# The mask product in four 32-column pieces, and the unread products at routing's end in 64-row halves

## The chip, the cores and the metric

The kernel runs on one core of a Trainium2 chip. A core has a matrix engine (TensorE, PE in the profile, with its weight loads as PEld), VectorE (DVE), ScalarE (ACT), GpSimd (POOL) and SyncE (SP), which issues most of the DMA transfers. The metric is the device time of one execution in microseconds (us); lower is better. Three runs of the kernel before took 480.1, 476.44 and 481.21 us, a median of 480.1.

## What is computed

An attention over 8 batches of 8 heads, 576 positions and 64 channels is the sum of two softmax attentions. One works on queries, keys and values averaged over groups of four positions, and its result is repeated four times. The other is local: a position sees only positions less than four away. The result, 4608 rows of 512, goes through a layer of experts. A row whose skip score is positive goes to the expert of its largest logit and adds that expert's two-layer output, weighed by the softmax of its logits; the other rows stay as they are.

```python
mask = np.abs(pos[:, None] - pos[None, :]) < factor          # factor = 4
scores = scale * np.matmul(q, k.transpose(0, 1, 3, 2))
scores = np.where(mask, scores, -1000000000.0)
...
out[do_compute] = xc + y      # y = gate * relu(xc @ w1[e]) @ w2[e]
```

## The kernel before

**Attention.** The 4608 rows are cut into 36 tiles of 128, each made of four groups of 32 positions. A group sees a window of 38 keys, so a tile's local scores are 128 x 304 (8 heads of 38) in one bank of PSUM, a tile S of which there are two. `scores` (line 409) makes them: first one product of the bf16 identity `idb` with the mask `mk`, 128 x 128 weights and 304 moving columns, which writes zeros and large negative numbers into the whole bank; then 16 products in fp32, for four pairs of heads and four groups, each with 32 columns of weights, that add queries times keys into their 32 partitions. A product in fp32 shows in the trace as two passes, so the 16 stand there as x32. `s_max` and `s_sub` on VectorE read the bank. The averaged attention (names ending in d: KD, qd, Ed, PTd), the values (`O<-VB,PT`, `O<-vd,PTd`, products of 32 columns) and the repeated result (`O<-U,rep`, full products) are mixed between.

**Order.** All steps up to the experts are entries of a list (`node`), and the table `ORDER` says in which order they are written. PE, ACT and DVE, and likewise POOL and SP, carry them out in that order, each engine in its own queue. Loads of the next batch are tied to the product that was written last ahead of them (`paced`), so that the queue of SP waits for PE.

**Routing.** After every 16 tiles, and once more after the last four, `route` turns the logits into lists of rows for each expert. On VectorE the last call finds each row's expert (oh), counts (on PE, `Sd<-oh,tri` and `Sd<-oh,ones`), makes the slot of each row (sl, s_all, blk, smod, ok), the number of rows of each expert (cnt), and two factors of a list product, Am and Bm. PE multiplies them (`Sd<-Bm,Am`), VectorE adds the result to ids and writes gix, the row numbers by expert. With gix POOL fetches the rows of the first expert (`xr<-out,gix`, three fetches of 128 rows), PE transposes them, ACT and DVE split them in two, and the experts' products begin. Gate weights follow the same way in a second list product with 72 columns.

**Unread products.** Among these last steps stand four entries `warm_s` (line 911), which multiply a tile of ones by itself into a bank S whose content nobody reads, 2, 2, 4 and 4 times with 512 columns (`WARM`). Behind the table's part 14 more of the kind stand between the first transposes (`WARMX`, into `py`).

**Steps that the table does not place.** Behind the experts the kernel has a branch for experts with more than 384 rows. Its condition is worked out by five VectorE steps, nf and nb (lines 1088 to 1092), from cnt. They are written after the hand-set order ends, and the planner of the language puts them where its own reckoning of time suggests; in the kernel before they stand among the steps that make gix.

Of the kernel before, what the change touches and what calls it, by code (L numbers as in the profile page):

```python
# [12 lines left out]
F32 = mybir.dt.float32  # L13
# [9 lines left out]
H, SEQ, HD = 8, 576, 64  # L23
E, D, F = 8, 512, 1024
QG, KW = 32, 38
# [7 lines left out]
WV = KS * KR  # L33
CAP = 384
NBK = CAP // 128
WARM = (2, 2, 4, 4)
WARMX = (5, 4, 3, 2)
SR = 8192
C_RANK, C_COL, C_BASE, C_SP8, C_SP4, C_SP2 = 0, 8, 32, 48, 56, 60
# [83 lines left out]
def tile_attention_moe(ctx, tc, qT, kT, vW, v4, mask, cst, ups, cid, w9, w1, w2, out):  # L123
    nc = tc.nc
# [3 lines left out]
    def pool(stack, name, bufs, **kw):  # L128
        return stack.enter_context(tc.tile_pool(name=name, bufs=bufs, **kw))
# [5 lines left out]
    ident = cp.tile([128, 128], F32, name="ident")  # L135
# [17 lines left out]
    psS = pool(att, "psS", 2, space=PSUM)  # L153
# [6 lines left out]
    mk = kvp.tile([128, 4, KW], BF16, name="mk")  # L160
    idb = kvp.tile([128, 128], BF16, name="idb")
# [15 lines left out]
    quad = [slice(32 * j, 32 * j + 32) for j in range(4)]  # L177
# [16 lines left out]
    def mm(*args, **kw):  # L194
        last[:] = [nc.tensor.matmul(*args, **kw)]  # L195
# [213 lines left out]
    def scores(i):  # L409
        S = psS.tile([128, 512], F32, name="S")  # L410
        Sv = TT[i]["S"] = S[:, :H * KW].rearrange("p (h k) -> p h k", h=H)
        v = MASKS.get(i % 9, 0)
        mm(Sv, lhsT=idb, rhs=mk[:, v:v + 1, :].to_broadcast([128, H, KW]), start=True, stop=False)
        for p in range(4):
            for j, b, g in groups(i):
                o, k = SEQ * p + QG * g, KO + SEQ * p + QG * g - 3
                mm(Sv[quad[j], 2 * p:2 * p + 2], lhsT=B[b]["Q"][:, o:o + QG],
                                 rhs=KBs[b % 2][:, :, k:k + KW], start=False, stop=p == 3)
# [338 lines left out]
    def node(fn, *args):  # L757
        nodes.append((fn, args))
# [55 lines left out]
    for b in range(NB):  # L814
# [39 lines left out]
        for i in range(NTILE):  # L854
            if (4 * i + 3) // NG != b:
                continue
            if i % 2 == 0 and i > 0:
                for r in range(2):
                    node(load_v, i // 2, r)
            node(scores, i)  # L860
            node(s_max, i)
            node(s_sub, i)
# [19 lines left out]
            if i % RG == RG - 1 or i == NTILE - 1:  # L882
                n = i % RG + 1
# [23 lines left out]
    def warm(t, n):  # L907
        for _ in range(n):
            nc.tensor.matmul(t, lhsT=ones, rhs=ones[:, None, :].to_broadcast([128, 4, 128]), start=True, stop=True)

    def warm_s(n):
        warm(psS.tile([128, 512], F32, name="S"), n)

    for e in range(2):
        node(load_n, e)
    for n in WARM:
        node(warm_s, n)
# [176 lines left out]
    with tc.If(some > 0):  # L1094
# [11 lines left out]
        for e in range(E):  # L1106
            n_blk = nc.values_load(nb[0:1, e:e + 1], engines=engines, min_val=0, max_val=(NTOK - CAP + 127) // 128)
            with tc.If(n_blk > 0):
# [7 lines left out]
                with tc.For_i(0, n_blk, 1) as it:  # L1116
# [14 lines left out]
                    for f in range(8):  # L1131
                        ph = psV.tile([128, 512], F32, name="pho")
                        for c in range(4):
                            nc.tensor.matmul(ph[:, :128], lhsT=w1t[:, f // 2, c, 128 * (f % 2):128 * (f % 2) + 128],
                                             rhs=xt[:, c, :], start=c == 0, stop=c == 3)
# [78 lines left out]
```

## Time and profile before

| | |
|---|---|
| three timed runs | 480.1, 476.44, 481.21 us |
| the profiled execution | 477.29 us |
| its span, from first to last instruction | 475.5 us |
| granted TensorE clock, mean over the span | 0.983 of full |
| PE busy | 437.1 us (92%) |
| DVE busy | 314.8 us (66%) |
| ACT busy | 252.9 us (53%) |
| POOL busy | 169.8 us (36%) |

Busy shares are means over stages: attention lasts until about 197 us, routing's end until about 226 us, the experts until the end. A product's time in the trace runs from its first column to the end of its result, and the next product starts well before that, so that what a product costs PE is read from start to start.

### The profile page before, as it was taken

The page shows a single profiled execution, that of the slowest core. Times are in us where ns is not written, and L with a number is a line of the kernel's source. Part 1 is how long each engine was busy: PE and PEld are TensorE (multiplying, and loading weights), DVE is VectorE, ACT ScalarE, POOL GpSimd, SP SyncE. Part 2 cuts the span into 40 slices and gives each one's busy share as a digit, 9 for nine tenths or more (in the row PEclk, how much of TensorE's full clock was granted, in tenths as well). Part 3 has the DMA queues.
Part 4 walks back from the last instruction along what each step waited for, and adds up shares of the span by engine and source line. Part 5 has one row for each costly group of instructions (what it writes and reads, how often), then busy time and mean ns, then how long its engine had stood idle before and what let it go on. Part 6 is the DMA issues. An engine that isn't in the chain of part 4 may idle for free. (4 is left out here: it accounts for less than half of the span.)

```text
span 475.5 us, 13311 instructions
## 1 busy us (share of the span) xinstructions
PE 437.1 (92%) x5461; PEld 366.6 (77%) x5461; DVE 314.8 (66%) x573; ACT 252.9 (53%) x585; POOL 169.8 (36%) x191
## 2 busy tenths in 40 slices
PE   0879989899999999997999999999999999999990
PEld 0557767678787777783898989989989899899880
DVE  4899987668779879575546555546686644776330
ACT  7547777587767678643443443344646334363210
POOL 8575967346567346005200502304131220202001
PEclk9989999999999999997999999999999999999997
DMA  7888879788898786653835544645776664555101
GB/s 259 275 257 272 278 230 287 217 253 299 253 287 282 222 252 221 176 180 107 274 132 179 206 142 152 197 161 163 244 225 241 204 214 130 181 180 193 47 4 60
DMA packets 27116, 96.71 MB, mean 203 GB/s; under 512 B 4245, under 2 KB 4629, under 8 KB 24618
## 3 DMA queue, kind: packets, MB, share of 16 engines
q1 hardware_dynamic: 23186, 84.36, 56.3%
q0 software_dynamic: 3840, 11.09, 6.4%
q8 instruction: 64, 1.05, 0.9%
q14 instruction: 26, 0.21, 0.1%
HBM read 81.20 MB, written 15.73 MB: 204 GB/s over the span
## 5 line engine op out<-in xcount | busy, mean ns | idle before, releaser
L958 POOL DMA_INDIRECT out<-Y,six x24 | 24.2, 1010 | 189.9 <-DVE Y L1018 188.1
L991 PE MATMUL ph<-xth,w1h 128*128 128x384 f32 (+2 forms) x256 | 80.6, 315 | 0.3 <-ACT xth L982 0.3
L991 PE MATMUL ph<-xtl,w1h 128*128 128x384 f32 (+2 forms) x256 | 78.9, 308 | 0.3 <-DVE xtl L983 0.3
L991 PE MATMUL ph<-xth,w1l 128*128 128x384 f32 (+2 forms) x256 | 78.8, 308 | 0.0
L1011 PE MATMUL py<-w2h,hh 128*128 128x512 f32 x168 | 66.1, 394 | 0.4
L1011 PE MATMUL py<-w2h,hl 128*128 128x512 f32 x168 | 65.7, 391 | 0.0
L1011 PE MATMUL py<-w2l,hh 128*128 128x512 f32 x168 | 65.5, 390 | 0.0
L1000 ACT ACTIVATE hh<-ph 128x384 fp32r<-128x384 f32 x64 | 30.7, 490 | 55.4 <-PE py L1011 27.8
L1001 DVE SCALAR_TENSOR_TENSOR hl<-ph,hh 128x384 fp32r<-128x384 f32 x64 | 34.7, 554 | 35.3 <-ACT hh L1000 35.3
L991 PEld LDWEIGHTS ph<-xth,w1h 128*128 128x128 f32 x256 | 48.1, 188 | 1.2 <-ACT xth L982 0.8
L991 PEld LDWEIGHTS ph<-xtl,w1h 128*128 128x128 f32 x256 | 48.3, 188 | 0.9 <-DVE xtl L983 0.5
L991 PEld LDWEIGHTS ph<-xth,w1l 128*128 128x128 f32 x256 | 48.1, 188 | 0.0
L288 DVE TENSOR_REDUCE KD<-KB 128x288 f32<-128x1152 f32 (+1 forms) x36 | 42.7, 1209 | 7.1 <-DMA KB<-kT 7.0
L709 DVE TENSOR_TENSOR w2l<-raw,w2h 128x1024 fp32r<-128x1024 f32 x32 | 39.1, 1221 | 10.4 <-ACT w2h L708 10.4
L982 ACT CAST xth<-Tx 128x512 fp32r<-128x512 f32 x22 | 13.0, 590 | 59.9 <-PE Tx L977 59.9
L747 DVE TENSOR_TENSOR w1l<-raw,w1h 128x1024 fp32r<-128x1024 f32 x30 | 36.7, 1225 | 7.8 <-ACT w1h L742 7.8
L445 POOL TENSOR_TENSOR Nt<-Et,r 128x304 f32<-128x304 f32 x36 | 25.9, 724 | 43.4 <-DVE r L442 12.6
L708 ACT CAST w2h<-raw 128x1024 fp32r<-128x1024 f32 x32 | 33.6, 1050 | 14.3 <-PE py L1011 14.3
L195 PE MATMUL O<-VB,PT 126*32 126x128 f32 x1152 | 38.6, 275 | 1.5 <-DMA VB<-vW 1.0
L195 PE MATMUL Sd<-KD,qd 128*128 128x288 f32 (+1 forms) x128 | 27.3, 422 | 13.1 <-DVE qd L268 11.8
L983 DVE TENSOR_TENSOR xtl<-Tx,xth 128x512 fp32r<-128x512 f32 x22 | 15.2, 692 | 36.1 <-ACT xth L982 36.1
L1011 PEld LDWEIGHTS py<-w2h,hl 128*128 128x128 f32 x168 | 31.5, 188 | 7.0
(155 smaller groups left out, 930.2 us busy)
## 6 DMA issues: line engine op xcount, KB each, us to landing
raw<-w SPq DMA_DIRECT2D x62, 512.0 KB
VB<-vW SPq DMA_DIRECT2D x36, 336.0 KB
Q<-qT SPq DMA_DIRECT2D x16, 576.0 KB
out<-X SPq DMA_DIRECT2D x36, 256.0 KB
KB<-kT SPq DMA_DIRECT2D x14, 576.0 KB
V<-v SPq DMA_DIRECT2D x8, 640.0 KB
V<-v SPq DMA_DIRECT2D x8, 512.0 KB
KB<-kT SPq DMA_DIRECT2D x4, 288.0 KB
```

Of the source, the lines that this page charges most:

```text
L195: last[:] = [nc.tensor.matmul(*args, **kw)]
L288: i = nc.vector.tensor_reduce(out=kd, in_=kv, axis=AX.X, op=ALU.add)
L445: nc.gpsimd.tensor_tensor(out=Ns[i % NNS][:, :, :KW, :2], in0=TT[i]["E"], in1=heads(TT[i]["r"])[:, :, None, :].to_broadcast([128, 4, KW, 2 ...
L708: nc.scalar.copy(out=hf, in_=raw)
L709: nc.vector.tensor_tensor(out=flat(lo), in0=raw, in1=hf.bitcast(F32), op=ALU.subtract)
L747: nc.vector.tensor_tensor(out=flat(lo), in0=raws[e, j], in1=flat(hi).bitcast(F32), op=ALU.subtract)
L958: ins = nc.gpsimd.indirect_dma_start(bounds_check=NOUT - 1, oob_is_err=False, **kw).ins
L983: nc.vector.tensor_tensor(out=x["xl"][:, :, ks], in0=Tv, in1=x["xh"][:, :, ks].bitcast(F32), op=ALU.subtract)
L991: nc.tensor.matmul(P[i][:, :n], lhsT=a[:, c, 128 * i:128 * i + 128], rhs=bb[:, c, :n], start=m == 0, stop=m == 11)
L1000: nc.scalar.activation(out=hh[:, i], in_=p, func=AF.Relu)
L1001: nc.vector.scalar_tensor_tensor(out=hl[:, i], in0=p, scalar=0.0, in1=hh[:, i].bitcast(F32), op0=ALU.max, op1=ALU.subtract)
L1011: nc.tensor.matmul(py[k], lhsT=a[:, i, ks], rhs=bb[:, i, :], start=(j == 0 and i == 0 and m == 0), stop=(j == 3 and i == 1 and m == 2))
```

## The change

The mask product is cut in four: each has 32 columns of the identity as weights, moves the same 304 columns and writes its 32 partitions. The bank's content is the same. The four unread calls now write two banks S by turns, with fp32 pieces of the identity that have 64 rows, the upper and the lower half: the first and third call do it with 128 columns of weights and 128 moving columns, six products each, the second and fourth with 32 columns of weights and 64 moving columns, 24 products each.

```diff
-WARM = (2, 2, 4, 4)
+WARM = (0, 1, 0, 1)
...
-        mm(Sv, lhsT=idb, rhs=mk[:, v:v + 1, :].to_broadcast([128, H, KW]), start=True, stop=False)
+        for j in range(4):
+            mm(Sv[quad[j]], lhsT=idb[:, quad[j]], rhs=mk[:, v:v + 1, :].to_broadcast([128, H, KW]), start=True, stop=False)
...
     def warm_s(n):
-        warm(psS.tile([128, 512], F32, name="S"), n)
+        ts = [psS.tile([128, 512], F32, name="S") for _ in range(2)]
+        hs = [slice(64 * k, 64 * k + 64) for k in range(2)]
+        for _ in range(3):
+            for t, h in zip(ts, hs):
+                if n == 0:
+                    nc.tensor.matmul(t[:, :128], lhsT=ident[h], rhs=ident[h], start=True, stop=True)
+                else:
+                    for c in range(n):
+                        for j in range(4):
+                            nc.tensor.matmul(t[quad[j], 64 * c:64 * c + 64], lhsT=ident[h, quad[j]], rhs=ident[h, :64],
+                                             start=True, stop=True)
```

Here is PE at one tile in the middle of attention, where the mask stands behind values of 32 columns (VB, PT), before:

```order
L195 MATMUL O<-U,rep 128x512
L195 MATMUL O<-VB_119,PT 32x128 x16
L195 LDWEIGHTS idb
L195 MATMUL S<-mk,idb 128x304
L195 MATMUL S<-KB_116,Q 32x76 x16
```

And the same place in the changed kernel:

```order
L195 MATMUL O<-VB_119,PT 32x128 x16
L195 LDWEIGHTS idb
L195 MATMUL S<-mk,idb 32x304
L195 LDWEIGHTS idb
L195 MATMUL S<-mk,idb 32x304
L195 LDWEIGHTS idb
L195 MATMUL S<-mk,idb 32x304
L195 LDWEIGHTS idb
L195 MATMUL S<-mk,idb 32x304
L195 MATMUL S<-KB_116,Q 32x76 x16
```

One weight load and one product have become four of each; nothing else moved on PE in attention, and the rows of ACT, POOL and SP are those of before.

VectorE in the last call of `route`, from the slots of the last four tiles to gix, before:

```order
L654 TENSOR_TENSOR ok<-cs,blk 128x96
L890 TENSOR_TENSOR cnt<-BT,cs 128x8
L670 TENSOR_TENSOR Am<-cs,smod 128x512
L662 TENSOR_TENSOR Bm<-ok,pcs 128x4x48
L698 TENSOR_TENSOR acc<-Sd,acc 128x120
L1088 TENSOR_SCALAR nf<-cnt 128x8
L529 TENSOR_TENSOR ids<-acc 128x24
L1089 TENSOR_REDUCE nf<-nf 128x1
L685 TENSOR_TENSOR ids<-Sd,ids 128x24
L1090 TENSOR_SCALAR nf<-nf 128x8
L689 TENSOR_TENSOR gix<-Sd,ids 128x24
```

And in the changed kernel:

```order
L891 TENSOR_TENSOR cnt<-BT,cs 128x8
L1099 TENSOR_SCALAR nf<-cnt 128x8
L1100 TENSOR_REDUCE nf<-nf 128x1
L1101 TENSOR_SCALAR nf<-nf 128x8
L1102 CAST nb<-nf 128x9
L1103 TENSOR_SCALAR nb<-nb 128x8
L671 TENSOR_TENSOR Am<-cs,smod 128x512
L663 TENSOR_TENSOR Bm<-ok,pcs 128x4x48
L699 TENSOR_TENSOR acc<-Sd,acc 128x120
L530 TENSOR_TENSOR ids<-acc 128x24
L686 TENSOR_TENSOR ids<-Sd,ids 128x24
L690 TENSOR_TENSOR gix<-Sd,ids 128x24
```

The five steps nf and nb, of which three stood among ids and gix and two behind gix, now stand together between cnt and Am. No line of the diff says so: the planner placed them anew.

PE around the first unread call, between the list products of an earlier round (Am, 120 columns) and the counts (tri, ones), before:

```order
L195 MATMUL Sd<-Bm,Am 128x120
L909 LDWEIGHTS ones
L909 MATMUL S<-ones 128x512
L909 LDWEIGHTS ones
L909 MATMUL S<-ones 128x512
L195 LDWEIGHTS tri
```

And in the changed kernel:

```order
L195 MATMUL Sd<-Bm,Am 128x120
L918 MATMUL S<-ident 128x128 x6
L195 LDWEIGHTS tri
L195 MATMUL Sd<-oh,tri 128x45
L195 LDWEIGHTS ones
```

The call keeps its place; two products of 512 columns have become six of 128, and in the second and fourth call two and four have become 24 of 64.

## Rows read from the trace of the kernel before

**Rows 1.** Windows: stretch, its length, busy time (and instructions) of each engine, clock, DMA.
```profile
42.00:86.00 44.00, 39.12 (x881) 29.73 (x872) 38.75 (x85) 31.42 (x102) 32.28 (x35) 1.00 0.84 257
86.00:197.00 111.00, 108.51 (x2405) 85.82 (x2407) 85.82 (x188) 82.09 (x242) 58.13 (x65) 1.00 0.84 257
...
213.74:220.57 6.83, 5.28 (x24) 2.25 (x23) 4.84 (x30) 1.22 (x5) 2.43 (x4) 0.52 0.14 35
226.00:475.50 249.50, 237.31 (x1357) 214.46 (x1356) 139.29 (x172) 102.09 (x148) 45.30 (x42) 0.99 0.51 168
```

**Rows 2.** Timeline of PE in attention: start, length, operation, count; merged where equal.
```profile
42.56 0.31 PE L195 MATMUL S<-mk,idb 128*128 128x304 bf16 x1
...
104.92 0.74 PE L195 MATMUL S<-KB,Q 128*32 128x76 f32 x32
105.59 0.50 PE L195 MATMUL O<-U,rep 128*128 128x512 f32 x1
...
107.43 0.31 PE L195 MATMUL S<-mk,idb 128*128 128x304 bf16 x1
107.67 0.73 PE L195 MATMUL S<-KB,Q 128*32 128x76 f32 x32
108.22 1.05 PE L195 MATMUL O<-xS,w9t 128*32 128x128 f32 x32
109.20 0.51 PE L195 MATMUL O<-U,rep 128*128 128x512 f32 x1
...
182.14 0.30 PE L195 MATMUL S<-mk,idb 128*128 128x304 bf16 x1
```

**Rows 3.** Waits of PE from 30 to 205 us: total, times, longest.
```profile
PE S L195 <- issue: 2.9, 1, 2.9
PE O L195 <- DMA VB<-vW: 1.0, 1, 1.0
PE Sd L195 <- DVE KD L288: 0.9, 1, 0.9
```

**Rows 4.** Waits of SP's DMA queue from 42 to 197 us, longest first.
```profile
SPq L239 <- PE T L198: 27.7, 11, 5.5
```

**Rows 5.** Timeline at routing's end, all engines; in brackets idle time ahead and its releaser.
```profile
211.95 0.59 PE L909 MATMUL S<-ones 128*128 128x512 bf16 x2
...
213.07 0.18 PE L195 MATMUL Sd<-oh,tri 128*128 128x45 bf16 x1 [0.53 <-DVE oh L591]
...
213.67 0.20 DVE L637 TENSOR_TENSOR sl<-sl,oh 128x36 f32<-128x36 f32 x1
...
213.90 0.19 DVE L642 TENSOR_REDUCE s_all<-sl 128x4 int32<-128x36 f32 x1
...
214.51 0.16 DVE L890 TENSOR_TENSOR cnt<-BT,cs 128x8 int32<-128x8 f32 x1
214.59 0.69 DVE L670 TENSOR_TENSOR Am<-cs,smod 128x512 bf16<-128x512 f32 x1
...
215.61 0.34 PE L195 MATMUL Sd<-Bm,Am 128*128 128x48 bf16 x4 [1.23 <-DVE Bm L662]
215.77 3.59 PE L909 MATMUL S<-ones 128*128 128x512 bf16 x8
...
216.27 0.18 DVE L689 TENSOR_TENSOR gix<-Sd,ids 128x24 int32<-128x24 f32 x1
...
219.15 0.45 PE L195 MATMUL Sd<-Bm,Am 128*128 128x72 bf16 x4
...
225.00 0.63 PE L977 MATMUL ph<-ident,xr 128*128 128x128 f32 x4 [0.76 <-DMA xr<-out,gix]
```

**Rows 6.** Timeline of PE: unread products at full clock, between transposes.
```profile
223.44 0.81 PE L909 MATMUL py<-ones 128*128 128x512 bf16 x3
```

**Rows 7.** Tile S: durations in ns, min/median/max, first and last start.
```profile
L195 PEld LDWEIGHTS S<-KB,Q x1152: 105/109/178, 13.1 to 197.3; 128*32 128x32 f32 x192
...
L909 PE MATMUL S<-ones x12: 376/631/632, 211.9 to 218.7; 128*128 128x512 bf16 x12
```

## The prediction

> **What bounds the kernel now.** I read the windows first, then PE's timeline, what PE waits for, and last routing's end. The windows [rows 1] show two long stages with PE on top: attention from 86 to 197 us (PE busy 108.51 of 111.00, no other engine over 86) and the experts from 226 us on (237.31 of 249.50). From 42 to 86 us PE (39.12 of 44.00) and DVE (38.75) are level. The change touches no expert instruction, so that stage can only start earlier or later. A busy PE is not a PE at its peak; so the reader is to look next at start-to-start times in its timeline [rows 2]. In the view of waits PE stops seldom in attention: its longest waits are 2.9 us on an issue, 1.0 on the load of VB, 0.9 on KD [rows 3]. The loads themselves are held back by PE (27.7 us of one queue's waits are for transposes [rows 4]), so a PE that is ahead draws them ahead. At routing's end [rows 5] PE is not the bound: a row of DVE steps leads to gix, with it POOL fetches rows, and the experts begin once the third fetch has landed and is transposed (225.00, behind 0.76 of waiting for it).
>
> **Part 1: the mask product, 36 times.** First the price of going from products of 32 columns to one of 128. Scores (KB, x32) with another 32-column group behind them take 0.55 us, 107.67 to 108.22; with a full product behind them 0.67, 104.92 to 105.59 [rows 2]. So a switch costs about 0.12. Then the mask's own streaming: three unread products of 512 columns take 0.81 and one lasts 0.38 [rows 6, 7], so they start (0.81 - 0.38) / 2 = 0.215 apart, and 304 columns stream in 0.128. From mask to scores the timeline has 0.24 (107.43 to 107.67): 0.128 and a switch back.
>
> Where a mask stands behind a 32-column group its slot is now 0.12 + 0.24 = 0.36 and becomes 0.13 if the four products run side by side; I take 0.20 saved and not 0.23, since all these starts are rounded to 0.01 and a switch may be nearer to 0.10. Where it stands behind a full product, the switch only moves from behind the mask to ahead of it, and nothing is saved. In PE's timeline 22 of the 36 masks stand behind a 32-column group: 2 before 30 us, 8 from 42.56 to 82, 12 from 88 to 182.14 (first and last of these 20 in [rows 2]).
>
> That the four run side by side has its model in the products behind them: 32 passes of 128 columns take 0.98 us less one switch (108.22 to 109.20), 0.107 for each four, and 128 columns at two cycles in fp32 are 0.107. Weight loads hide the same way: each lasts 0.109 and 32 go by in 0.55 us [rows 2, 7].
>
> A rule speaks against this. The Trainium skill, "TensorEngine Tiling (Array Packing)", Restrictions and Gotchas, says that column tiling excludes Fast Weight Load, so the four bf16 loads would go the slow way where one 128-column load could go fast. The trace's 32-column loads in fp32 show no cost of their own between products. By the rows the sum is the one below; by the rule, with loads that nothing hides, it is rival D's.
>
> What survives: 22 x 0.20 = 4.4 us is the ceiling. The 2 early ones I drop, because DVE is busy there and PE often idle. Of the 8 up to 82 us (1.6) I keep half, 0.8: DVE is level with PE, and the wait for VB takes what was gained ahead of it; the 2.9 us wait behind them I let move along, since loads follow PE. Of the 12 later ones (2.4) I keep 2.0: nine fall ahead of the next long wait (KD), and short ones behind it take two gains. Together **-2.8**, with -4.4 at one end and -0.5 at the other (loads that follow nothing, rival B).
>
> **Part 2: five DVE steps change places.** The order shows what the diff does not: the steps nf to nb, which only an overflow needs, stood among ids and gix; now all five stand between cnt and Am. Before, cnt starts at 214.51 and Am 0.08 behind it [rows 5]. The five hang on each other, and a small step that hangs on the one ahead starts 0.23 behind it (sl 213.67, s_all 213.90). So Am starts 5 x 0.22, or 1.1 us, later, and all that hangs on it follows: Bm, the list products (215.61, which had waited 1.23 for Bm), gix (216.27), the fetches, the transposes at 225.00. Taking the five away from ids and gix gives nothing back, because gix hangs on the list products, which came in the middle of them. PE, POOL and ACT all wait for this chain, so nothing covers it. **+1.1**; ends 0 (if they fit into holes as before, rival A) and +1.2.
>
> **Part 3: the unread products.** They were 2, 2, 4 and 4 of 512 columns and are 6, 24, 6 and 24 in fp32 of 64 rows. A pass of 128 columns takes 0.107 (above), a product two passes, 0.215. No row shows two halves of 64 rows at once; the ends are six in a row (1.3 us) and three pairs (0.65). I take pairs, as nearest to the 32-column groups that do run together; the halves write two different banks.
> First call: its hole runs from 211.95 to the counts at 213.07, which wait for oh: 1.1 us. Three pairs and two switches need 0.9, free. Six in a row need 1.5 and push the counts by 0.4. DVE takes the counts up about 0.1 later than it could have, so +0.3. Second call: 24 of 64 columns, four abreast, need 0.65 at most and two switches; the list products behind it feed an acc that DVE reaches over 1 us later: nothing. Third and fourth call, at half clock: 1.3 and 0.65 with pairs, twice that without. Before, eight products stood 3.59 us from 215.77, and the last lists came behind them at 219.15. With Part 2 the third call begins near 216.9, and pairs are over by 219.0; without pairs by 221. The work behind (clearing banks, first transposes) has the time until the third fetch, now 225.00 + 1.1. What is late next is that fetch, so this is worth nothing either way. **0**; ends -0.1 and +0.3.
>
> The clock: from 213.74 to 220.57 the granted clock is 0.52 on average, so 1.2 GHz nearly throughout, after a stretch in which PE worked on products of 9 columns and idled for oh; from 226 us on it is 0.99 [rows 1]. I assume that it is at 2.4 GHz again before the experts.
>
> **Sum.** -2.8 + 1.1 + 0 = -1.7 us. The profiled execution took 477.29 (span 475.5 and 1.8 around it), so 475.6 against that one. It lies 2.8 below the median of the timed runs, 480.1, which spread over 4.8. The four known times (476.44, 477.29, 480.1, 481.21) have a mean of 478.8, and for a new median I forecast 478.8 - 1.7 = **477.1**. Chance 0.50.
>
> **Rivals**, from the same 478.8.
> A. All of it comes through: PE is the bound, loads follow it, and DVE's five steps fit into holes. For: PE 98% busy from 86 us on. Against: the 1.23 us in which the lists waited for Bm. -4.4: 474.4. Chance 0.17.
> B. The masks are covered: loads land when they land, and PE waits longer for VB and KD. For: a DMA share of 0.84 [rows 1]. Against: the queue waits for PE, not PE for it. -0.5 + 1.1 = +0.6: 479.4. Chance 0.15.
> C, on the other side: with fewer columns streamed in calls three and four the clock stays at half into the experts. Before, the eight products began at 215.77 and the clock rose at 220.57, 4.8 us on; dense expert work that has to run as long at half speed loses 2.4. With +0.3 of Part 3, +1.1 of Part 2 and only 2.0 of Part 1 that is +1.8: 480.6. It decides if the granted clock is 0.50 at the first w1 product. Against: the 14 products into py behind the table are still there. Chance 0.13.
> D. The split doesn't do what it says: the four products or their loads go one after another. 4 x 0.128 = 0.51 a slot, 0.15 more than the 0.36 behind 32-column groups and, with the switch ahead, 0.39 more than the 0.24 elsewhere: 22 x 0.15 + 14 x 0.39 = 8.8, of which I let 0.7 stay: 6.2, and 1.1: 486.1. Against: every 32-column group in the trace. Chance 0.05.
>
> **Numbers.** A measurement of this kernel can tell about 1% (4.8 us) from no change. The forecast's own range is 475 to 479. With A below and C above, 473.5 to 481 leaves out D and the tails. Faster by over 1%, under 475.3: most of A and a sixth of the forecast, 0.20. Slower by over 1%: D and a little of C, 0.06. Within: 0.74.
>
> **What would show it.** Part 1: four mask products that start a few ns apart, scores 0.13 behind the first, and no pause between VB or scores and the mask; behind full products a switch ahead of it. The last scores, now at 197.3 [rows 7], come 2.8 earlier. Part 2: cnt to Am 1.2 us where it was 0.08, and cnt to gix 2.9 where it was 1.76. Part 3: the counts still begin when oh is there. I am wrong if PE's waits for loads grow by what the masks give up, if the four masks start 0.13 apart, or if the clock is at 0.50 when the experts begin.

## The result and the profile after

The changed kernel is slower: 483.75 us median against 478.23 for the kernel before in the same runs, a ratio of 1.0141 with a 95% interval of 1.0111 to 1.0171. The forecast was 477.1, with a range of 473.5 to 481. The profiled execution of the changed kernel has a span of 482.2 us and took 483.99; before it was 475.5 and 477.29. Of the runs told of below, the profiled executions of a256 and m216 were disturbed ones and serve for the order of events, not for lengths of stages.

First the windows of the changed kernel, for the stretches of [rows 1]; the third is the one in which the granted clock was at half, the last the experts.

```profile
42.00:86.00 44.00, 40.12 (x1003) 32.94 (x995) 39.50 (x85) 32.86 (x105) 31.64 (x34) 1.00 0.85 267
86.00:197.00 111.00, 105.44 (x2374) 86.13 (x2370) 86.30 (x188) 80.55 (x238) 57.85 (x64) 0.98 0.80 253
210.40:230.88 20.48, 14.14 (x170) 10.15 (x168) 8.69 (x40) 3.97 (x10) 9.48 (x10) 0.50 0.43 130
...
233.00:482.20 249.20, 237.25 (x1356) 214.40 (x1356) 139.57 (x173) 102.03 (x148) 42.54 (x39) 0.98 0.50 164
```

The experts take as long as before (249.2 us with PE busy 237.25). PE has 3 us less to do from 86 to 197 us (105.44, was 108.51), and yet the stage ends where it ended. And 20.48 us at a granted clock of 0.50 (1.2 GHz) stand where there were 6.83 of mostly half (without the stop that is told of below it is 10.2 to 13.7 us in the changed kernel's variants).

Then tile S, the answer to [rows 7]: durations in ns, minimum, median and maximum, first and last start.

```profile
L195 PE MATMUL S<-KB,Q x1152: 227/228/334, 12.9 to 197.1; 128*32 128x76 f32 x192
L195 PE MATMUL S<-mk,idb x144: 291/301/461, 12.6 to 196.5; 128*32 128x304 bf16 x144
```

The last scores start at 197.1 and not 197.3: of the 2.8 us that Part 1 promised, 0.2 to 0.3 are there in this pair of executions. Now routing's end, all engines, the answer to [rows 5] (in brackets idle time ahead and what ended it).

```profile
212.72 1.65 PE L918 MATMUL S<-ident 64*128 64x128 f32 x12
...
213.31 0.20 DVE L592 TENSOR_TENSOR oh<-eq,pm 128x36 bf16<-128x36 f32 x1
...
214.30 0.22 PE L195 MATMUL Sd<-oh,tri 128*128 128x45 bf16 x1
...
215.72 0.16 DVE L891 TENSOR_TENSOR cnt<-BT,cs 128x8 int32<-128x8 f32 x1
...
216.80 0.68 DVE L671 TENSOR_TENSOR Am<-cs,smod 128x512 bf16<-128x512 f32 x1
...
218.49 0.18 DVE L690 TENSOR_TENSOR gix<-Sd,ids 128x24 int32<-128x24 f32 x1
...
218.96 1.23 POOL L969 DMA_INDIRECT xr<-out,gix  x1 [5.13 <-DVE z L600]
...
219.79 0.97 PE L922 MATMUL S<-ident 64*32 64x64 f32 x48
...
220.83 0.52 PE L195 MATMUL Sd<-Bm,Am 128*128 128x72 bf16 x4
221.10 0.14 PEld L910 LDWEIGHTS <-ones 128*128 128x128 bf16 x1
221.96 1.00 POOL L969 DMA_INDIRECT xr<-out,gix  x1 [0.30 <-issue]
...
225.49 0.23 DVE L699 TENSOR_TENSOR acc<-Sd,acc 128x72 f32<-128x72 f32 x1 [4.71 <-remote]
...
225.77 2.29 PE L910 MATMUL py<-ones 128*128 128x512 bf16 x5 [4.42 <-DVE acc L699]
```

Up to the third fetch the chain is 1.2 to 1.5 us late: cnt at 215.72 for 214.51, the third fetch at 221.96 for 220.47. The large loss comes behind that. The second list product starts at 220.83 and its last part at 221.10; VectorE's acc, which waits for it, starts at 225.49. "remote" says that the profile found nobody behind the wait; the semaphore events show that PE's answer for the last part arrived at 225.46. Before, acc came 0.29 behind the last part (219.34; it stands merged in the row of 219.15):

```profile
219.15 0.45 PE L195 MATMUL Sd<-Bm,Am 128*128 128x72 bf16 x4
...
219.63 0.23 DVE L698 TENSOR_TENSOR acc<-Sd,acc 128x72 f32<-128x72 f32 x1 [1.04 <-PE Sd L195]
...
220.47 1.00 POOL L958 DMA_INDIRECT xr<-out,gix  x1 [0.30 <-issue]
```

In the changed kernel PE itself then waits for acc with its first product into py, ACT clears ph from 225.81, and the last transposes, bound by the third fetch before (225.00), now come at 231.74. I call the lateness of acc, 4.1 us (4.39 less 0.29), **the stop**. From cnt to the first w1 product of the experts it is 17.4 us here (215.72 to 233.15), and 11.9 before.

### The profile page after: what moved, and what is told of

Its sections match the earlier page's. It is cut to its first block, busy times and chain, and to the rows that moved or that the text cites. A ratio compares the mean times of both kernels' runs of the same rounds, so it can differ in the third digit from the quotient of the medians.

```text
span 482.2 us, 13742 instructions
## 1 busy us (share of the span) xinstructions
PE 437.5 (91%) x5677; PEld 374.4 (78%) x5677; DVE 317.4 (66%) x573; ACT 253.3 (53%) x585; POOL 171.0 (35%) x191
## 3 DMA queue, kind: packets, MB, share of 16 engines
q8 instruction: 65, 1.06, 1.0%
## 5 line engine op out<-in xcount | busy, mean ns | idle before, releaser
L710 DVE TENSOR_TENSOR w2l<-raw,w2h 128x1024 fp32r<-128x1024 f32 x32 | 39.1, 1221 | 10.3 <-ACT w2h L709 10.2
L195 PE MATMUL Sd<-KD,qd 128*128 128x288 f32 (+1 forms) x128 | 28.8, 432 | 14.0 <-DVE qd L268 11.7
L195 PEld LDWEIGHTS O<-VB,PT 126*32 126x32 f32 x1152 | 30.2, 109 | 9.1 <-issue 7.4
```

Source lines behind the costliest of these rows:

```text
L710: nc.vector.tensor_tensor(out=flat(lo), in0=raw, in1=hf.bitcast(F32), op=ALU.subtract)
```

## Experiments

**Does the loss belong to the program, and to the place of its code?** While PE stood, one packet of a queue that carries instructions was under way. The DMA view of the changed kernel, whole span and then the 0.2 us from 221.6 (packets, MB, share of 16 engines):

```profile
q8 instruction: 65, 1.06, 1.0%
```

```profile
q0 software_dynamic: 18, 0.05, 66.0%
q8 instruction: 1, 0.02, 30.8%
```

Its packets are of 16384 bytes, and in attention 26 to 27 of them come for 6720 to 6879 records of PE, one for about 256 (a record is a weight load or a product's pass): this is PE's code. The change makes PE's program up to the first branch 8733 records long, from 8301. So I moved the code, by small products at PE's very start, where it idles until 11.38 us. A label's number is that of the records added (four to a product); the letter is the kernel: a the changed one, b the one before, m the mask pieces alone, w the new unread products alone.

```diff
     for k in ORDER:
         fn, args = nodes[k]
         fn(*args)
+        if fn is make_identity:
+            ts = [psS.tile([128, 512], F32, name="S") for _ in range(2)]
+            for m in range(20):              # a80
+                nc.tensor.matmul(ts[m // 4 % 2][quad[m % 4], :8], lhsT=ident[:, quad[m % 4]], rhs=ident[:, :8], start=True, stop=True)
```

Expected of a80: 

> The changed kernel, with 20 unread products of 32 columns of weights and 8 moving columns added at PE's very start, where it idles until 11.4 us. They cost nothing there but shift all later PE code by 80 records. Theory F (code fetch): in the changed kernel PE stood from the last list product (221.10 us) until 225.46, with one of its code fetches of 16384 bytes starting at 221.70; fetches come about every 256 PE records, so 80 records move that piece's edge to the start of the fourth unread call. By F the 4.4 us between last list product and acc shrink to 0.3 and the time falls by about 4 us, to 1.000 to 1.004 of the kernel before. Rival U (the unread products themselves, with the clock at half, cause the stop): the stop stays, 1.012 to 1.016 of the kernel before.

Of a160: 

> The same with 40 such products, 160 records, which move the edge into the second unread call, in front of the list products that lead to gix. F: no stop at acc; if an edge stops PE wherever it is short of code, a stop of up to 4 us could show at the second call or the lists behind it, and then gix comes late by that; I expect 1.000 to 1.006 of the kernel before. U: as the changed kernel, 1.012 to 1.016.

Measured 0.9981 (0.9944 to 1.0019) and 0.9967 (0.9932 to 1.0003). The stop is gone in both; in a80:

```profile
220.58 0.40 PE L195 MATMUL Sd<-Bm,Am 128*128 128x72 bf16 x4
220.73 0.14 PEld L910 LDWEIGHTS <-ones 128*128 128x128 bf16 x1
221.02 0.23 DVE L699 TENSOR_TENSOR acc<-Sd,acc 128x72 f32<-128x72 f32 x1 [0.49 <-PE Sd L195]
```

Then the changed kernel itself once more, and moved by one whole piece of code. Expected of again: 

> The changed kernel itself, unaltered, beside the runs with shifted code. If its loss of 1.4% and the stop of 4.1 us ahead of acc belong to the program, both come back: 1.012 to 1.017, and PE's last list product answers 4 us late. If they belonged to the place or the hour of the first measurement, it now runs like a80 and a160: 0.996 to 1.001 and no stop.

Of a256: 

> The changed kernel with 64 small products at PE's start, 256 records, one whole piece of code: every later edge falls where it falls in the changed kernel. F: the stop is back, 1.010 to 1.016. If small products at the start cure it by something else than the place of the code (an earlier start of PE, its clock): 0.996 to 1.001, like a80 and a160.

Both lose: 1.0113 (1.0043 to 1.0182) and 1.0113 (1.0059 to 1.0167). The stop is in both, here in again (in a256 acc stands 4.37 behind the last part):

```profile
216.88 0.40 PE L195 MATMUL Sd<-Bm,Am 128*128 128x72 bf16 x4
217.10 0.10 PEld L910 LDWEIGHTS <-ones 128*128 128x128 bf16 x1
...
221.49 0.23 DVE L699 TENSOR_TENSOR acc<-Sd,acc 128x72 f32<-128x72 f32 x1 [4.67 <-remote]
```

So small products at the start cure nothing by themselves; where the code stands does. Nor did the planner move anything between these runs: VectorE, ScalarE, GpSimd and SyncE have the same steps in the same order in the changed kernel, in all runs with the letter a, and in tail below. Rival U, that the unread products at half clock make the stop, falls: a80 has the same products, at a granted clock of 0.50 as well.

**How sharp is the place?** Expected of a8: 

> The changed kernel with two small products at PE's start, which move its later code by 8 records. The runs a80 and a160 showed that the stop of 4.4 us ahead of acc goes when the code stands 80 or 160 records further on. This asks how sharp that is. If the stop belongs to the edge of a 16384-byte piece that falls just behind the last list product, 8 records bring the edge among the list products or the last unread ones: the stop stays in some form, 3 to 5 us and 1.008 to 1.016 of the kernel before. If it hangs on one exact record, it is gone: 0.996 to 1.003.

Of a40: 

> The same with 10 products, 40 records: half way to a80. If what counts is that the edge is reached while rows are being fetched (from about 220.6 us), the edge now falls into the fourth unread call at about 219.5, and the stop is smaller or gone, 0.996 to 1.008. If any edge in or behind the fourth unread call stops PE, it stays, 1.010 to 1.016.

Of a248: 

> 62 small products, 248 records, which is one whole piece less 8: the edge stands 8 records later than in the changed kernel, behind the first unread product into py. If an edge there stops PE, the stop now shows between the py products or at the first transposes, where PE has a few us in hand before the third fetch: 1.000 to 1.012. If it hangs on one exact record: 0.996 to 1.003.

Of a4: 

> One small product at PE's start: the code edge stands 4 records earlier than in the changed kernel, within the last list products. If the stop belongs to a few records around the edge: it is there, 1.008 to 1.016. If it hangs on the exact record behind the last list product: 0.996 to 1.003.

Of a252: 

> 63 small products: the edge stands 4 records later than in the changed kernel, among the first unread products into py that wait for acc. If a few records around the edge count: 1.008 to 1.016, perhaps in the form of a later stop between these products. If it hangs on the exact record: 0.996 to 1.003.

Measured: a252 1.0019 (0.9979 to 1.0058), a248 0.9977 (0.9924 to 1.0030), a4 1.0055 (1.0016 to 1.0095), a8 1.0075 (1.0029 to 1.0121), a40 1.0013 (0.9966 to 1.0060). No profile of the five has the stop; acc stands 0.29 to 0.30 behind the last part in each. Four records either way were enough in these profiles. That a4 and a8 are still a little slow (2.6 and 3.6 us) is not explained by their one profile each, and whether the stop comes in some of their other executions is not shown. The granted clock, which is known of every execution, averages 0.969 to 0.971 in the three runs with the stop, 0.980 in a8 and 0.975 in a4, so that a8 looks free of it and a4 is open.

**What stands behind the last list product?** tail leaves all code ahead and puts eight small products behind the last list product:

```diff
+    ts = [psS.tile([128, 512], F32, name="S") for _ in range(2)]
+    for m in range(8):
+        nc.tensor.matmul(ts[m // 4 % 2][quad[m % 4], :8], lhsT=ident[:, quad[m % 4]], rhs=ident[:, :8], start=True, stop=True)
     att.close()
```

Expected: 

> The changed kernel with 8 small unread products (32 records) behind the last list product; all code ahead of them keeps its place, and they wait for nothing. If PE stops at the edge itself, the last list product is answered 4 us late as before, and the time stays at 1.010 to 1.016. If the stop needs a product that waits for another engine as the first behind the edge, the list product is answered within 0.3 us and the time is 0.996 to 1.003.

Measured 1.0034 (0.9992 to 1.0076), and no stop: acc at 221.68, the last part at 221.39. So the stop goes when products that wait for nothing follow at once. That it needs a waiting product as the next thing in PE's queue is the likely reading, from one run.

**Does it need both halves of the change?** w216, b176 and m216 have the last list product on the same record of a piece as a256 (228 of 256, counted from PE's first record; in the changed kernel it is 229).

Expected of w216: 

> The new unread products alone, with the old mask product; 54 small products at PE's start stand in for the records that the four mask pieces add, so that PE's code has the same place at routing's end as in the changed kernel, to one record. If the stop comes from the place of the code, it is there without the mask pieces: 1.012 to 1.017. If the mask pieces take part in it some other way, or it needs the exact record, the time is that of Part 2 alone: 1.1 us, 1.002.

Of b176: 

> The kernel before with 44 such products at PE's start, 176 records, which put its code's edge as many records ahead of the last list product as it has in the changed kernel. F: a stop like that of the changed kernel appears between the last list product and acc, and the time grows by 3 to 4.4 us, 1.006 to 1.009 of the kernel before. U, or a stop that needs the change: nothing, 0.998 to 1.002.

Of m216: 

> The mask in four pieces with the old unread products, and 54 small products (216 records) at PE's start, so that the record behind the last list product has the same place in its piece of code as in the changed kernel. If the place alone makes the stop: 1.006 to 1.012, and the last list product is answered 4 us late. If the stop needs the 96 quick records of the fourth unread call ahead of it: no stop, and the time is that of Part 1, which the attention stages of the runs so far put at 0.7 us: 0.994 to 1.000.

Measured: w216 0.9981 (0.9940 to 1.0022), b176 0.9953 (0.9920 to 0.9985), m216 0.9961 (0.9929 to 0.9992), and no stop in any. With b176 and w216 I had expected one. The place of the code is necessary, then, but not enough: with the old mask or the old unread products the same record brought nothing.

**Part 1 alone, and the small products alone.** Expected of m40: 

> The mask product in four pieces alone, with the old unread products; 10 products at PE's start make PE's code longer by 256 records in all, so that its edges lie at routing's end as in the kernel before, and the five steps nf to nb stand as before. The prediction's Part 1: 2.8 us faster (0.994), with 4.4 and 0.5 as ends. Rival B (loads cover it): 0.5 (0.999).

Of b256: 

> The kernel before with 64 small products (256 records, one whole piece) at PE's start. All later edges stay in their places. If b176's 0.5% came from where the edges stand: nothing here, 0.998 to 1.002. If it came from the small products at the start themselves (PE at work from 2.4 us on): 0.994 to 0.997, and then 2 us have to be allowed for in all comparisons of runs with such products.

Measured: m40 0.9989 (0.9949 to 1.0030), b256 0.9992 (0.9959 to 1.0024). So the small products by themselves cost and give nothing that these intervals can show, and b176's 0.5% is not theirs; where it comes from is open. m40 and m216 are 0.5 and 1.9 us faster than the kernel before; 2.8 (0.994) lies just outside the interval of the one and inside that of the other. But each is within 0.1% of the run of the old mask with the same place of the code at routing's end (b256 for m40, b176 for m216). No gain of Part 1 in time is shown.

**Part 2 undone**, with a160's place of the code:

```diff
-                nc.vector.tensor_tensor(out=gix, ...)
+                slot_i[:] = [nc.vector.tensor_tensor(out=gix, ...)]
...
-    nc.vector.tensor_scalar(out=nf[:, :E], in0=cnt, ...)
+    i = nc.vector.tensor_scalar(out=nf[:, :E], in0=cnt, ...)
+    tc.add_manual_dep(i.ins, slot_i[0].ins.name, ...)
```

Expected: 

> a160 with the five steps nf to nb tied behind gix, so that Am follows cnt at once: Part 2 undone, the stop absent. By the prediction it is 1.1 us faster than a160 (which had 0.9967 of the kernel before), so 0.9945; between cnt and gix 1.8 us where a160 has 2.8. If the third fetch is held by something else than gix, nothing: 0.997. This is also the candidate for a version faster than both kernels.

Measured 0.9972 (0.9934 to 1.0010), the same as a160. In the profile the step is undone as meant: cnt 207.89, Am 208.18, gix 209.87. A gain of 0.8 us is below what these intervals can show. No version here is shown to beat the kernel before by more than half a per cent.

## Why the prediction was wrong

**What failed first: the sum had no term for PE's code.** Part 3 said of the second list product and of all behind it "nothing", and "What is late next is that fetch, so this is worth nothing either way". With the stop it is the list product's answer that is late, by 4.1 us, and behind it PE and ACT do their clearing and transposing at half clock (from acc to the first w1 product 7.3 to 7.7 us where there were 6.7 before, and 6.4 to 7.2 in the changed kernel without the stop). That makes 4.8. From cnt to the first w1 product the three profiles with the stop take 17.4 to 17.7 us, the eight of the changed kernel without it (a4 to a252 and tail) 12.0 to 12.7, on average 5.2 less. The three runs with the stop average 1.0122, those eight 1.0015; times 478.2 that is 5.8 and 0.7 us, 5.1 apart. The stop is the loss. Shown is that it goes with 4 records more or less ahead of PE's later code and is back with 256, goes when products that wait for nothing follow the last list product, and did not come with either half of the change alone on the same record. Not shown is what PE lacks in it. A missing piece of code was my reading (theory F), and for it speaks that in the changed kernel and in a256 the list products themselves already stutter (0.52 and 0.64 us where a80 has 0.40). Three things speak against it. In again they do not stutter (0.40), and the stop is there. The piece seen under way starts 0.6 us behind the last part in one execution, 0.1 ahead of it in another and 1.0 ahead in the third, and the stop lasts 4.4 to 4.5 in all three, so that its landing alone does not end it. And the edge of a piece is not where F put it: by the pauses of attention, told of below, it lies 36 to 38 records ahead of the last list product, in the fourth unread call, which runs through without a pause (219.79, 0.97 us for its 48 passes). The cause of the stop stays open.

**Part 1: the mechanism right, what survives not clear of nothing.** The four mask products mostly start 3 to 7 ns apart, scores 0.13 to 0.14 us behind the first, and behind a 32-column group there is no pause; rival D is out. PE in the changed kernel, first two masks behind 32-column groups:

```profile
92.37 1.08 PE L195 MATMUL O<-VB,PT 126*32 126x128 f32 x32
93.27 0.31 PE L195 MATMUL S<-mk,idb 128*32 128x304 bf16 x4
93.40 0.71 PE L195 MATMUL S<-KB,Q 128*32 128x76 f32 x32
93.92 0.31 PE L195 MATMUL S<-mk,idb 128*32 128x304 bf16 x4
...
110.47 0.31 PE L195 MATMUL S<-mk,idb 128*32 128x304 bf16 x4
110.61 0.70 PE L195 MATMUL S<-KB,Q 128*32 128x76 f32 x32
111.13 0.39 PE L195 MATMUL O<-vb,PTd 128*32 128x128 f32 x7
113.43 0.30 PE L195 MATMUL O<-vb,PTd 128*32 128x128 f32 x1 [1.90 <-issue]
```

The whole gain is there in PE's work, and much of it is lost again: to pauses like the one of 1.90 us in the last row, and to stretches at half clock. From the ninth tile's scores to the last tile's, in us, as means over the profiles (four with the whole mask, twelve with the four pieces, without a256 and m216). Idle time counts where no product runs; of a stretch at half clock, half its length counts as lost:

| | whole | four pieces |
|---|---|---|
| PE at work, at full clock | 149.4 | 144.8 |
| PE waits for nothing shown | 3.3 | 4.5 |
| other idle time | 4.0 | 4.5 |
| lost to stretches at half clock | 0.0 | 1.3 |
| length (lowest, highest) | 156.7 (154.2, 159.2) | 155.0 (149.7, 157.9) |

The work falls by 4.6. In this stretch 20 masks stood behind a 32-column group, and 20 times 0.23 is 4.6; I had taken 0.20. Of that, 1.7 is left in the length, where I kept 2.8. But single lengths scatter by 2 to 3 us, and the difference of the two means is uncertain by about 1.4 (one standard error), so that 1.7 is told apart neither from nothing nor from 2.8; the 1.2 of the second row is no surer. Sure is the work, which scatters by 0.4 to 0.7.

The second row of the table is what I misread. My prediction let the 2.9 us wait on an issue [rows 3] "move along, since loads follow PE". Here it is in the kernel before, in the middle of a tile's scores:

```profile
81.88 0.72 PE L195 MATMUL S<-KB,Q 128*32 128x76 f32 x28
85.51 0.33 PE L195 MATMUL S<-KB,Q 128*32 128x76 f32 x4 [2.90 <-issue]
```

The 28 passes ahead of it read the same tiles, so it is no load. A piece of PE's code starts at 83.15, 2.36 us ahead of the end of that pause; in the changed kernel one starts at 110.84, 2.59 ahead of 113.43. In all eighteen profiles there are 84 pauses of PE over 0.15 us in this stage that no semaphore explains, and every one ends 2.2 to 3.5 us behind the start of such a piece, 79 of them within 2.2 to 2.85, while the pieces themselves come 3.4 to 10.7 us apart. All 84 also stand at one place of the code: counted in PE's records, each comes at the same record of 256, to one record, in all eighteen profiles, however many records were put ahead. So place and time both say that this is the edge between two pieces, and that PE stands there because its code is late. The mask pieces add 216 records to attention, nearly one more piece. Whether pauses grow at all, and whether by these records or by a PE that reaches each edge sooner, the runs do not tell apart. The Trainium skill, "Runtime: NRT & Kernel Launch", Instruction fetch mechanics, says that code comes in blocks of 16 KiB, the next one fetched while the present one runs, and that this is mostly hidden. The trace agrees on the size (16384 bytes), and on the word mostly: of the 474 pieces of this stage in the eighteen profiles some 390 brought no pause. What is left is not small here, 3.3 and 4.5 us of attention on average.

**Part 2 as forecast, a little smaller.** cnt to Am is 1.08 us (forecast 1.2) and cnt to gix 2.77 (2.9). From cnt to the third fetch it is 6.24 or 6.25 in eleven of the twelve profiles with the five steps together, and 5.4 to 5.5 in four of the six without; so +0.8 for the +1.1. In the kernel before and in m40 POOL took its first fetch 1.4 us behind gix, where it is 0.5 otherwise (0.9 in a8), and the third at 6.0, so against that one execution only 0.3 shows.

**Part 3, the unread products themselves.** The row halves run in pairs as I took them: starts 7 ns apart, and the next pair 0.11 us later at full clock (a8), 0.21 at half. The counts do not always begin when oh is there: from oh to tri it is 0.34 us before, in a8, in tail and in n160, where the clock fell only behind the first call, but 0.98 or 0.99 in the changed kernel and seven others, where it had already fallen when the first call began (0.68 and 0.82 in a160 and w216, where it fell during the call). The old first call takes 1.06 us at half clock and still fits (b176 and b256, 0.34); the new one takes 1.65. The step that failed here is that I priced the first call at full clock alone. Forecast 0, with an end of +0.3; it was 0 to +0.65.

**The other rivals.** B gave 479.4, +0.6; the stop-free runs lie there (+0.7), but by luck, since B's loads are not what covers the gain: idle time that is no pause for code rises by only 0.5 us in the table. C does not hold as it was put: the granted clock is 0.50 until 230.88, but full again when the first w1 product starts at 233.15. A is out. Without the stop the terms as measured, -1.7, +0.8 and about +0.4, make -0.5 us, and the eight stop-free runs average +0.7; the 1.2 between them is within what the runs can tell. Against such runs the forecast would have stood inside its range, but no run shows its gain.

## What to carry to other kernels

A wait "on issue" in the middle of a group of products is worth a look at the queue that carries instructions: if a piece of code starts some 2.4 us ahead of its end, PE waits for its code, and a change that makes PE's work shorter by using more and smaller instructions may lose part of its gain there. When a change adds records to PE's program, run it also with the later code moved by a few dozen records at an idle place; without such a control, a loss of a per cent that comes and goes with the place of the code is put down to the change itself. And where single executions of a stage differ by 5 us, compare its parts over many profiles (work, pauses, clock), not its end in two.

## What the runs showed of the hardware that was not expected

- PE's code arrives in packets of 16384 bytes, one for about 256 records, and PE stood 1.1 to 6.2 us per execution for it in attention (a256 left out); a pause ends 2.2 to 2.85 us behind the packet's start in 79 of 84 cases, and all 84 come at the same record of 256, to one record, with PE's later code moved by 0 to 256 records.
- A few records decide: in the changed kernel, as it is or moved by 256 records, the last list product stands on record 229 or 228 of 256 (counted from PE's first), and its answer came 4.1 us late in all three profiles, on records 224 and 232 it did not, nor on 229 when unread products that wait for nothing followed it. With the old mask or the old unread products record 228 brought nothing, and an edge of PE's code, as the pauses show it, lies 36 to 38 records ahead.
- Two fp32 products of 64 rows, in the upper and the lower half, run side by side: starts 7 ns apart, pairs 0.107 us apart with 128 columns at a granted clock of 1.0 and 0.213 at 0.50.
